# A fused attention and mixture-of-experts kernel: the first stage's unsplit result kept in a buffer of its own, and one more tile made with seven products

## The chip, the cores and the metric

One core of a Trainium2 chip runs the whole kernel in one launch. The metric is the device time in microseconds (us), from the first to the last instruction plus what lies around them. The profile also gives the *span*, the time from the first to the last instruction of one profiled execution.

## The reference, cut to what matters

```python
x = attention(q, k, v, proj)                    # hash-bucket masked, 1536 tokens x 512
x = moe(x, w_gate, w_output_gate, w1, w2)       # 8 experts, relu, 512 -> 1024 -> 512   ("first stage" below)
def _moe2_ref(x, w_a, w_b, w_out):              # ("second stage" below)
    a = x @ w_a                                 # 512 -> 1536
    b = x @ w_b
    return (a * b @ w_out).astype(np.float32)
```

## The kernel before, in words

The kernel has three parts, one behind another: attention, the experts (the first stage here), and the gated product `a * b @ w_out` (the second stage here). The change touches the end of the first stage and the second stage.

**Split operands.** Every matmul works on pairs: a value is written as a rounded high part (`ACT.activation(..., Copy)` into fp32r) plus a low part (value minus high part, on VectorE or GpSimd), and a product is three matmuls, high*high, high*low, low*high (`mm3`, L910 to L913; `product`, L1151; `outp`, L1077).

**The experts** loop over 8 experts `e` and 8 blocks `f`. In each step TensorE does `mm1(e, f)` and then `mm2` of the step before; ScalarE makes the relu's high part (L924), VectorE the low part (L925), and `mm2` needs both one step later. When an expert is done, `y_sum` (one step into the next expert) adds two PSUM halves into `yt`, and `y_store` (two steps in) splits `yt` into its high part `y_h` (four ScalarE copies, L975) and its low part `y_l` (four on VectorE, L976). The last expert is split straight from PSUM by `y_evac` (L957, L958). `y_h` and `y_l` hold 4 blocks of 128 channels by all tokens; GpSimd zeroes them before the first store (L814).

**The second stage** goes over 12 blocks `f` of the 1536 hidden columns, and for each over two halves `c` of 768 tokens: 24 tiles (c, f). For f < 2 a tile is *plain* (`ab`): two token halves `hf` of 384, each 8 weight blocks by 3 matmuls into two PSUM banks, `aba` and `abb`; that is 48 matmuls. From f = 2 on a tile is made with *seven* products (`seven`, a Winograd-type scheme): 7 products by 2 by 3 = 42 matmuls, with VectorE sums between them (L1171, L1175). It alternates the banks from tile to tile (`turn`). Seven products need sums of the activations, `TH` and `TL`, made once for each c by `t_work`: the unsplit value is first put together again as `y_h + y_l` (L1117, `whole`), then come the differences (L1120), the rounded high parts on ScalarE (L1123) and the low parts on VectorE (L1127). The intermediate sums lie in the buffer `accs`, which later holds output sums. They also need sums of the weights (`s_work`, L1142 to L1147).

**Side work.** Each tile has steps in which it hands out other work: `fill(k)` takes one `outp` (three 512-wide matmuls of the output product, for a tile made before), `side(k)` takes what `todo_of` laid down for step k: turning the raw 64-bit weights into floats (`w2_a` on ScalarE, `w2_s` on VectorE, `w2_k` on ScalarE, `w2_b` on VectorE, then the next load on SP's queue), splitting weights (`part`: L881 on ScalarE, L882 on GpSimd; `w2_c` for the output weights), weight sums. In a plain tile `ab` first issues all matmuls of a token half, then the copy of `aba` (L1068), the product with `abb` (L1069), the rounding (L1052), and only then come steps 0 to 2 (first half) or 3 to 6 (second half). A step of a plain tile also takes one item from `todo`, the list of all `t_work` items: 28 steps, 28 items. The low part of `a * b` (L1054, `low`) is issued when the next half's matmuls have been issued.

The order on every engine is the program's order: an instruction that waits holds all behind it on its engine. A buffer that is used again waits for the last use of what it held, also for a use that comes later in the program on another engine.

Of the kernel before, what the change touches and what calls it, by code (L numbers as in the profile page):

```python
# [23 lines left out]
C = 224  # L24
# [9 lines left out]
def attn_moe_kernel(ctx: ExitStack, tc: tile.TileContext, xin, cst, projd, wblk, wmoe, w2in, out):  # L34
# [567 lines left out]
    with tc.manual_schedule():  # L602
# [214 lines left out]
        s2 = ctx_2.enter_context(tc.tile_pool(name="s2", bufs=3, reuse_waits="tile"))  # L817
# [10 lines left out]
        SEQ = [(0, 0), (0, 1), (1, 0), (1, 1), (0, 2)]  # L828
        for m in range(2, 12):
            SEQ += [(m, 0), (m, 1), (m - 1, 2)]  # L830
# [10 lines left out]
        def w2_a(*k):  # L841
            T2[k] = c2.tile([128, 512], F32, tag="t2", name="t2", bufs=5)
            f64_hi(R2[k], T2[k])

        def w2_s(*k):
            X2[k] = c2.tile([128, 512], U32, tag="x2", name="x2")
# [16 lines left out]
        def w2_c(m):  # L863
            t = T2.pop((m, 2))
            h = s2.tile([128, 512], F32R, tag="h2", name="h2")
            l = s2.tile([128, 512], F32R, tag="l2", name="l2")
# [4 lines left out]
        SW = {}  # L871
# [5 lines left out]

        def part(m, nm):
            src = SW[nm] if nm in SW else a_part(m, nm)
            p = s2.tile([128, 2, 256], F32R, tag="pc", name="pc", bufs=9)  # L880
# [103 lines left out]
        def cc_work():  # L984
# [20 lines left out]
            (7, 7): [ids_load],  # L1005
# [3 lines left out]
        for n, (e, f) in enumerate(steps):  # L1009
            mm1(e, f)  # L1010
            if n:
                mm2(*steps[n - 1])
            if f == 0 and e:
                y_sum(e - 1)
            w_split(n + 2, 0)
            w_split(n + 1, 1)
            if f == 1 and e:
                y_store(e - 1)
            if f in (4, 6) and e + 1 < E:
                x_tpose(e + 1, (f // 2 - 2,))  # L1020
            if f == 6 and e + 2 < E:
                x_load(e + 2)
            if e == E - 4 and f in (2, 4, 6):
# [19 lines left out]
        accs = fast.tile([128, 9, 512], F32, name="accs")  # L1043
        af = accs.rearrange("p a b -> p (a b)")
# [13 lines left out]
        def ab(c, f, hf):  # L1058
# [3 lines left out]
            order = [(i, d) for k in range(2) for i in range(2) for d in (2 * k, 2 * k + 1)]  # L1062
            for i, d in order if first else sorted(order):
                    pc = PCS[f, f"{i + 1}{d // 2 + 1}"]
                    wh, wl = (pc[:, k, d % 2 * 128:d % 2 * 128 + 128] for k in range(2))
                    mm3(p[i][:, :384], wh, wl, y_h[:, d, t0:t0 + 384], y_l[:, d, t0:t0 + 384], d == 0, d == 3)
            a = tmp(("c11", "c21")[hf])
            ACT.activation(a, p[0][:, :384], ACTF.Copy)  # L1068
# [5 lines left out]
        def outp(k, f):  # L1074
# [16 lines left out]
            o = accs[:, (k - 6) % 9]  # L1091
            if own:
                o = s2.tile([128, DM], F32, tag="pc", name="osb", bufs=9)
                ACT.activation(o, a, ACTF.Copy, scale=s)
            elif f == 1:
# [15 lines left out]
        def t_work(c):  # L1111
            yh, yl = y_h.bitcast(F32), y_l.bitcast(F32)
            at = ((3072, 0, 768, 1536), (2304, 0, 768, 1536))[c]
            t1, t2, t3, t4 = TF = [af[:, o:o + 768].rearrange("p (a b) -> p a b", a=2) for o in at]

            def whole(o, d, n):
                return lambda: DVE.tensor_tensor(out=o, in0=yh[:, d, n], in1=yl[:, d, n], op=ALU.add)  # L1117

            def tt(o, x, y, op=ALU.subtract):
                return lambda: DVE.tensor_tensor(out=o, in0=x, in1=y, op=op)  # L1120

            def hi(i):
                return lambda: ACT.activation(TH[c][i], TF[i], ACTF.Copy)  # L1123

            def low(i):
                th = TH[c][i].bitcast(F32) if i else yh[:, lo_d, n2[c]]
                return lambda: DVE.tensor_tensor(out=TL[c][i], in0=TF[i], in1=th, op=ALU.subtract)  # L1127

            a, b = n1[c], n2[c]
# [6 lines left out]
        def s_work(m, k):  # L1136
            def new(nm):
                SW[nm] = fast.tile([128, 256], F32, tag=nm, name=nm)
                return SW[nm]

            if k == 0:
                DVE.tensor_tensor(out=new("s1"), in0=a_part(m, "21"), in1=a_part(m, "22"), op=ALU.add)  # L1142
                DVE.tensor_tensor(out=new("s2"), in0=SW["s1"], in1=a_part(m, "11"), op=ALU.subtract)
            elif k == 1:
                DVE.tensor_tensor(out=new("s3"), in0=a_part(m, "11"), in1=a_part(m, "21"), op=ALU.subtract)
            else:
                DVE.tensor_tensor(out=new("s4"), in0=a_part(m, "12"), in1=SW["s2"], op=ALU.subtract)  # L1147
# [15 lines left out]
        def seven(c, m, fill, side, low):  # L1163
# [40 lines left out]
            c21 = add(tmp("c21"), y, p1)  # L1204
# [9 lines left out]
        def todo_of(c, f):  # L1214

            m, w = [[] for _ in range(7)], []
            if c == 0:
                w = [(2, f)]
                if 1 <= f < 11:
                    for k, at in ((0, 4), (1, 4), (2, 5)):  # L1220
                        m[at].append(lambda k=k: s_work(f + 1, k))
            elif f < 10:
                w = [(0, f + 2), (1, f + 2)]
            for k, (i, n) in enumerate(w):
                m[2 * k].append(lambda a=(n, i): w2_a(*a))
                m[2 * k + 1] += [lambda a=(n, i): w2_s(*a), lambda a=(n, i): w2_k(*a)]
                m[2 * k + 2].append(lambda a=(n, i): w2_b(*a))
            if c == 0:
                m[3].append(lambda: w2_c(f))
            elif f < 11:  # L1230
                for k, nm in enumerate(ORDER if f else ("11", "12", "21", "22")):
                    m[k].append(lambda nm=nm: part(f + 1, nm))
# [11 lines left out]
        ts = [t_work(c) for c in range(2)]  # L1244
        todo = ts[0][0] + ts[1][0]
        low = None
        for f in range(12):
            for c in range(2):
# [10 lines left out]
                if f < 2:  # L1259
                    for hf in range(2):  # L1260
                        last, low = low, ab(c, f, hf)
                        if last:
                            last()
                        for k in ((0, 1, 2), (3, 4, 5, 6))[hf]:
                            fill(k)
                            side(k)
                            if todo:
                                todo.pop(0)()
                    if (c, f) == (0, 0):
                        cc_work()  # L1270
                    if f:
                        for g in ts[c][1]:
                            g()
# [70 lines left out]
```

## Time and profile before

| | |
|---|---|
| time, median of 3 runs | 743.83 us (743.38 to 744.12) |
| the profiled execution's own time | 742.49 us |
| its span | 740.7 us |
| TensorE's mean granted clock in it | 0.992 |
| first stage (experts) | to about 435.8 us |
| four plain tiles | about 435.8 to 487.3 us |
| twenty tiles of seven products | from 487.3 us |

A row of a timeline gives the start in us, the duration in us, the engine, the line of the kernel, what is written and read, and in brackets how long the engine sat idle before it and what released it. TensorE's rows overlap, since its matmuls are pipelined: the distance between two starts is the cost of one, the duration is not.

### The profile page before, as it was taken

Reading aid. Unit: us, or ns where it says so; the run is one execution under the profiler, and the core shown is the slowest. Engines: PE = TensorE matmul, PEld = TensorE weight load, DVE = VectorE, ACT = ScalarE, POOL = GpSimd, SP = SyncE. Lnnn points to the kernel's source line nnn. Section 1 sums busy time; section 2 is a strip of 40 time slices with the busy share of each in tenths; the row PEclk is TensorE's granted clock in tenths of the full one; section 3 lists DMA queues with packets and bytes.
Section 4 is the critical chain, followed back from the end, with each engine's and each line's share of the span. In section 5 each row is a group of like instructions: output and inputs, shape, how many; then the busy total and the mean of one; then the engine's idle time right before and its main releaser. Section 6 shows DMA issues by size and latency. Waiting matters only on the chain.

```text
span 740.7 us, 13120 instructions
## 1 busy us (share of the span) xinstructions
PE 715.0 (97%) x4561; PEld 612.0 (83%) x4562; DVE 554.2 (75%) x1099; ACT 439.6 (59%) x929; POOL 223.0 (30%) x261
## 2 busy tenths in 40 slices
PE   8899999999999999999999998799999999999995
PEld 6676777776776789999999997788999999999994
DVE  6778777888776678777778858866777777777653
ACT  6878777777777357666677745456443453434311
POOL 3233232333533283212210002133223332233215
PEclk9999999999999999999999999899999999999998
DMA  7357351321301068888898612121212212120003
GB/s 239 118 214 262 102 167 58 105 69 66 134 8 60 15 223 241 241 188 243 267 238 275 209 30 85 38 78 57 86 35 80 86 58 86 33 81 31 1 30 145
DMA packets 42681, 88.48 MB, mean 119 GB/s; under 512 B 7328, under 2 KB 10736, under 8 KB 42608
## 3 DMA queue, kind: packets, MB, share of 16 engines
q1 hardware_dynamic: 39936, 81.07, 35.5%
q0 software_dynamic: 2304, 6.31, 2.3%
q8 instruction: 38, 0.62, 0.4%
q14 instruction: 35, 0.29, 0.1%
q10 hardware_dynamic: 368, 0.20, 0.1%
HBM read 73.32 MB, written 13.12 MB: 117 GB/s over the span
## 4 chain that ended last, share of the span: by engine, by line
PE 79%; DVE 7%; issue 6%; ACT 3%; POOL 3%; DMA 2%; SPq 0%; POOLq 0%; ACTq 0%; DVEq 0%
PE tp L186 9%; PE av L201 8%; PE y L951 6%; PE s L158 4%; PE s L159 4%; PE h L913 4%; PE h L912 3%; PE h L911 3%; PE y L952 3%; PE aba L1156 3%; PE abb L1156 3%; PE aba L1158 3%; PE aba L1157 3%; PE abb L1158 3%; PE abb L1157 3%
## 5 line engine op out<-in xcount | busy, mean ns | idle before, releaser
L164 DVE TENSOR_REDUCE mm<-s 128x1 f32<-128x768 f32 x96 | 91.1, 949 | 25.1 <-PE s L159 24.1
L173 ACT ACTIVATE p<-s,sb 128x768 f32<-128x768 f32 x96 | 94.8, 988 | 21.7 <-DVE sb L165 21.0
L186 PEld LDWEIGHTS tp<-cs,p 128*128 128x128 f32 x576 | 64.2, 140 | 36.7 <-ACT p L173 23.4
L485 DVE TENSOR_TENSOR wl<-wr,wh 128x512 fp32r<-128x512 f32 x125 | 81.5, 692 | 8.4 <-ACT wh L484 3.1
L186 PE MATMUL tp<-cs,p 128*128 128x128 f32 x576 | 82.2, 279 | 4.8 <-ACT p L173 3.9
L190 ACT ACTIVATE pt<-tp 128x384 f32<-128x384 f32 x143 | 64.9, 487 | 32.6 <-PE tp L186 32.6
L484 ACT ACTIVATE wh<-wr 128x512 fp32r<-128x512 f32 x128 | 73.7, 623 | 3.2 <-DMA wr<-wmoe 3.0
L951 PE MATMUL y<-hl,wh 128*128 128x448 f32 x224 | 74.8, 377 | 0.1
L158 PE MATMUL s<-tk,tq 76*128 76x384 f32 x192 | 73.1, 381 | 0.3 <-DVE tq L135 0.3
L911 PE MATMUL h<-xh,wh 128*128 128x224 f32 x256 | 71.5, 279 | 0.2 <-ACT xh L418 0.2
L913 PE MATMUL h<-xh,wl 128*128 128x224 f32 x256 | 70.7, 276 | 0.2 <-DVE wl L485 0.2
L912 PE MATMUL h<-xl,wh 128*128 128x224 f32 x256 | 70.3, 274 | 0.3 <-DVE xl L419 0.3
L882 POOL TENSOR_TENSOR pc<-t,pc 128x256 fp32r<-128x256 f32 x38 | 30.0, 791 | 128.8 <-ACT pc L881 59.8
L201 PE MATMUL av<-pt,v 128*64 128x384 f32 x360 | 68.0, 499 | 0.2 <-DVE r L225 0.2
L1052 ACT ACTIVATE gh<-c 128x384 fp32r<-128x384 f32 x28 | 14.7, 526 | 88.2 <-DVE c L1175 67.8
L159 PE MATMUL s<-bk,bq 128*128 128x384 f32 x192 | 65.1, 339 | 0.0
L952 PE MATMUL y<-hl,wl 128*128 128x224 f32 x224 | 59.6, 266 | 0.0
L911 PEld LDWEIGHTS h<-xh,wh 128*128 128x128 f32 x256 | 49.0, 191 | 1.3 <-ACT xh L418 0.4
L913 PEld LDWEIGHTS h<-xh,wl 128*128 128x128 f32 x256 | 49.2, 192 | 0.4 <-DVE wl L485 0.4
L912 PEld LDWEIGHTS h<-xl,wh 128*128 128x128 f32 x256 | 49.2, 192 | 0.5 <-DVE xl L419 0.5
L201 PEld LDWEIGHTS av<-pt,v 128*64 128x64 f32 x360 | 21.9, 136 | 32.7 <-issue 24.5
L882 POOL TENSOR_TENSOR pc<-s,pc 128x256 fp32r<-128x256 f32 x40 | 36.0, 910 | 42.8 <-ACT pc L881 42.8
(235 smaller groups left out, 1921.9 us busy)
## 6 DMA issues: line engine op xcount, KB each, us to landing
wr<-wmoe SPq DMA_DIRECT2D x128, 256.0 KB
r<-w2in SPq DMA_DIRECT2D x36, 512.0 KB
x<-xin SPq DMA_DIRECT2D x30, 384.0 KB
xr<-zero SPq DMA_DIRECT2D x13, 512.0 KB
xg<-xr SPq DMA_DIRECT2D x14, 256.0 KB
v<-xin SPq DMA_DIRECT2D x16, 192.0 KB
wb<-wblk SPq DMA_DIRECT2D x1, 640.0 KB
x<-xin SPq DMA_DIRECT2D x3, 192.0 KB
```

The costliest lines, as they stand in the source:

```text
L158: PE.matmul(p[:, c, :384], T[h, 0][:76, qs], T[h, 1][:76, sl], start=True, stop=False)
L159: PE.matmul(p[:, c, :384], B[h, 0][:, qs], B[h, 1][:, sl], start=False, stop=True)
L164: DVE.tensor_reduce(out=m[:, 1:2], in_=st[g][:, :, :384], axis=AX.XY, op=ALU.min)
L173: ACT.activation(p.rearrange("p (c n) -> p c n", c=2), st.pop(g)[:, :, :384], ACTF.Exp, scale=scl.pop(g), bias=nbs.pop(g), accum_out=sums[ ...
L186: PE.transpose(ps[:, j * 128:(j + 1) * 128], pt_[g][:, k * 128:(k + 1) * 128], ident)
L201: PE.matmul(av[h][c * 64:(c + 1) * 64, :384], v, PT[h][:, k, c * 384:(c + 1) * 384], start=(k == 0), stop=(k == NT - 1), skip_group_check= ...
L485: eng.tensor_tensor(out=l, in0=r, in1=h.bitcast(F32), op=ALU.subtract)
L911: PE.matmul(ps, wh, xh, start=first, stop=False)
L912: PE.matmul(ps, wh, xl, start=False, stop=False)
L913: PE.matmul(ps, wl, xh, start=False, stop=last)
L951: PE.matmul(p, wh[:, w], hl, start=(f == 0), stop=False, skip_group_check=True)
L952: PE.matmul(p[:, 0], wl[:, w], hl[:, 0], start=False, stop=(f == 7), skip_group_check=True)
```

## The change: what it does

1. A third buffer `y_w` of the shape of `y_h` takes the unsplit first-stage result. Four more memsets on GpSimd zero it; `y_store` gets four more ScalarE copies for each of the first seven experts, and two ScalarE copies from PSUM serve the last.
2. `t_work` works in place on `y_w`: the sums `whole` go, and one difference fewer is made. The buffer `accs` goes; its output sums lie in parts of `y_w` that are no longer needed (`AT`).
3. The tile (0, 1) is made with seven products instead of plain. So the weight sums of block 1 are made at the end of the first stage (steps (7, 6) and (7, 7)), block 1 has eight weight parts instead of four, and the list `todo` is replaced by places written out by hand in `todo_of` for the tiles (0, 0), (1, 0), (0, 1), (1, 1) and (0, 2).
4. In a plain tile the steps are spread: the copy of `aba` is issued as soon as its last matmul is issued, then, in the middle of the matmuls, the `low` of the half before and step 0 or 3 (`mid`); steps 1, 2 or 4 to 6 come behind the rounding. The very first half calls `mid` behind its matmuls.
5. Buffers are smaller or elsewhere: raw weights 3 to 2, converted weights 5 to 4, sign bits 2 to 1, weight parts 9 in one pool to 4 + 5 in two. The order of weight loads (`SEQ`) and of `part` changes. `p1` also serves as the product buffer of the second half and of `c21`. One output sum (block 1, k = 4) is scaled on VectorE instead of ScalarE.

The diff, cut to its core (new tile pools and the moved `s_work`, `pc_tile` as described above are left out):

```diff
-        for y in (y_h, y_l):
+        y_w = yp.tile([128, 4, N + C], F32, name="y_w")
+        for y in (y_h.bitcast(F32), y_l.bitcast(F32), y_w):
             for d in range(4):
-                POOL.memset(y.bitcast(F32)[:, d], 0.0)
-        r2 = ctx_2.enter_context(tc.tile_pool(name="r2", bufs=3, reuse_waits="tile"))
+                POOL.memset(y[:, d], 0.0)
+        r2 = ctx_2.enter_context(tc.tile_pool(name="r2", bufs=2, reuse_waits="tile"))
...
-            T2[k] = c2.tile([128, 512], F32, tag="t2", name="t2", bufs=5)
+            T2[k] = c2.tile([128, 512], F32, tag="t2", name="t2", bufs=4)
...
-            w2_load(SEQ.index(k) + 3)
+            w2_load(SEQ.index(k) + 2)
...
             for d in range(4):
-                y = YS.pop((e, d))
+                y = YS[e, d]
                 ACT.activation(y_h[:, d, sl], y, ACTF.Copy)
                 DVE.tensor_tensor(out=y_l[:, d, sl], in0=y, in1=y_h.bitcast(F32)[:, d, sl], op=ALU.subtract)
+            for d in range(4):
+                ACT.activation(y_w[:, d, sl], YS.pop((e, d)), ACTF.Copy)
...
+            (7, 6): [lambda: s_work(1, 0)],
+            (7, 7): [ids_load, lambda: s_work(1, 1), lambda: s_work(1, 2)],
...
             y_evac(E - 1, i)
+        for i in range(2):
+            src = Y[E - 1][i].rearrange("p (a b) -> p a b", a=2)[:, :, :C]
+            ACT.activation(y_w[:, 2 * i:2 * i + 2, bass.ds(o_regs[E - 1], C)], src, ACTF.Copy)
...
-        def ab(c, f, hf):
+        def ab(c, f, hf, mid):
...
+            a = tmp(("c11", "p1")[hf])
             for i, d in order if first else sorted(order):
...
-            a = tmp(("c11", "c21")[hf])
-            ACT.activation(a, p[0][:, :384], ACTF.Copy)
+                if (i, d) == (0, 3):
+                    ACT.activation(a, p[0][:, :384], ACTF.Copy)
+                    if not first:
+                        mid()
+            if first:
+                mid()
...
+            elif f == 1 and k == 4:
+                DVE.tensor_scalar(out=o, in0=a, scalar1=s, scalar2=None, op0=ALU.mult)
...
+            w = (y_w[:, lo_d, a], y_w[:, hi_d, b], y_w[:, lo_d, b], y_w[:, hi_d, a])
...
             return [
-                whole(t3, lo_d, b), whole(t1, lo_d, a), tt(t1, t3, t1), whole(t2, hi_d, b), tt(t3, t2, t3),
-                tt(t2, t2, t1), tt(t4, yh[:, hi_d, a], t2), tt(t4, t4, yl[:, hi_d, a], ALU.add), hi(1),
-                hi(2), low(1), hi(3), low(2), low(3),
-            ], [hi(0), low(0)]
+                tt(w[0], w[2], w[0]), tt(w[2], w[1], w[2]), tt(w[1], w[1], w[0]), tt(w[3], w[3], w[1])
+            ] + [g(i) for i in (1, 2, 3, 0) for g in (hi, low)]
...
-            c21 = add(tmp("c21"), y, p1)
+            c21 = add(p1, y, p1)
...
+            if f < 3:
+                t, u = t_work(0), t_work(1)
+            if (c, f) == (0, 0):
+                before.extend(t[:3])
+                conv(0, 2, 0, 1, 1, 2)
+                for k, g in ((1, t[3]), (2, t[4]), (3, u[0]), (5, t[6]), (5, t[5])):
+                    put(k, g)
+                put(4, w2_c, 0)
+                for k, nm in ((0, "11"), (2, "s2"), (3, "12"), (4, "s3"), (6, "s1")):
+                    put(k, part, 1, nm)
+            elif (c, f) == (1, 0):
+                conv(1, 2, 0, 1, 1, 2)
+                for k, g in ((0, t[7]), (1, t[8]), (2, t[9]), (3, t[10]), (4, t[11])):
+                    put(k, g)
+                put(3, w2_c, 1)
+                for k, nm in ((4, "22"), (5, "s4"), (6, "21")):
+                    put(k, part, 1, nm)
+                put(6, cc_work)
+            elif (c, f) == (0, 1):
+                for k, g in ((0, u[1]), (1, u[2]), (2, u[3]), (5, u[4]), (6, u[6])):
+                    put(k, g)
+                conv(2, 0, 3, 4, 4, 5)
+            elif (c, f) == (1, 1):
+                conv(2, 1, 0, 1, 1, 2)
+                for k, g in ((0, u[5]), (1, u[7]), (3, u[8]), (4, u[9]), (6, u[10])):
+                    put(k, g)
+                for k in range(3):
+                    put(2 + k, s_work, 2, k)
+                conv(3, 0, 4, 5, 5, 6)
+                for k, nm in ((2, "11"), (3, "12"), (4, "s2"), (5, "s3"), (5, "s1"), (6, "22"), (6, "s4")):
+                    put(k, part, 2, nm)
...
-                if f < 2:
+                if f < 2 and (c or not f):
...
                     for hf in range(2):
-                        last, low = low, ab(c, f, hf)
-                        if last:
-                            last()
-                        for k in ((0, 1, 2), (3, 4, 5, 6))[hf]:
-                            fill(k)
-                            side(k)
-                            if todo:
-                                todo.pop(0)()
+                        def mid(last=low):
+                            if last:
+                                last()
+                            step(3 * hf)
+
+                        low = ab(c, f, hf, mid)
+                        for k in ((1, 2), (4, 5, 6))[hf]:
+                            step(k)
```

## Rows read from the trace of the kernel before

**Rows 1.** The page's part 1: busy time, share, instructions of each engine.
```profile
PE 715.0 (97%) x4561; PEld 612.0 (83%) x4562; DVE 554.2 (75%) x1099; ACT 439.6 (59%) x929; POOL 223.0 (30%) x261
```
**Rows 2.** Stretches: from:to, length, busy time and count of each engine, granted clock, DMA.
```profile
478.00:482.00 4.00, 4.00 (x13) 3.71 (x12) 1.14 (x3) 4.00 (x8) 2.21 (x3) 0.50 0.32 93
524.00:547.00 23.00, 23.00 (x121) 21.11 (x120) 18.15 (x33) 10.28 (x22) 6.88 (x8) 1.00 0.24 69
```
**Rows 3.** Timeline of TensorE, the plain tiles and the first of seven products.
```profile
435.87 0.42 PE L911 MATMUL aba<-y_h,pc 128*128 128x384 f32 x1
...
444.86 0.34 PE L911 MATMUL aba<-y_h,pc 128*128 128x384 f32 x1
...
451.00 0.34 PE L913 MATMUL aba<-y_h,pc 128*128 128x384 f32 x1
451.83 0.44 PE L911 MATMUL abb<-y_h,pc 128*128 128x384 f32 x1 [0.49 <-DVE c L1069]
...
453.88 0.34 PE L913 MATMUL abb<-y_h,pc 128*128 128x384 f32 x1
457.29 0.45 PE L911 MATMUL aba<-y_h,pc 128*128 128x384 f32 x1 [3.06 <-ACT c L1068]
...
473.12 0.40 PE L1086 MATMUL q<-l,gh 128*128 128x512 f32 x1
477.29 0.79 PE L1087 MATMUL q<-h,gl 128*128 128x512 f32 x1 [3.78 <-DVE gl L1054]
...
483.52 0.34 PE L913 MATMUL abb<-y_h,pc 128*128 128x384 f32 x1
...
485.27 0.39 PE L1085 MATMUL q<-h,gh 128*128 128x512 f32 x1
...
487.11 0.39 PE L1087 MATMUL q<-h,gl 128*128 128x512 f32 x1
487.33 0.33 PE L1156 MATMUL aba<-y_h,pc 128*128 128x384 f32 x1
...
491.57 0.44 PE L1156 MATMUL aba<-y_h,pc 128*128 128x384 f32 x1 [0.57 <-ACT p L1185]
...
494.50 0.44 PE L1156 MATMUL abb<-th,pc 128*128 128x384 f32 x1 [0.92 <-DVE u L1171]
...
500.93 0.34 PE L1156 MATMUL abb<-y_h,pc 128*128 128x384 f32 x1
...
503.09 0.44 PE L1156 MATMUL aba<-th,pc 128*128 128x384 f32 x1 [0.25 <-DVE u L1171]
```
**Rows 4.** Group of one line and shape, 433 to 501 us: busy, mean ns.
```profile
L1117 DVE TENSOR_TENSOR accs<-y_h,y_l 128x768 f32<-128x768 f32 x6 | 5.7, 951 | 0.0
```
**Rows 5.** Timeline of VectorE, then of GpSimd, in the plain tile (1, 0).
```profile
447.31 2.92 DVE L1120 TENSOR_TENSOR accs<-accs 128x768 f32<-128x768 f32 x2
...
447.10 1.33 POOL L868 TENSOR_TENSOR l<-t,h 128x512 fp32r<-128x512 f32 x1 [32.19 <-ACT h L867]
```
**Rows 6.** Timeline of ScalarE at two expert boundaries, and TensorE and VectorE at the last.
```profile
291.26 0.36 ACT L924 ACTIVATE hl<-h 128x224 fp32r<-128x224 f32 x1 [1.26 <-PE h L913]
...
419.81 1.22 ACT L975 ACTIVATE y_h<-yt 128x224 f32 x4
420.93 0.33 ACT L924 ACTIVATE hl<-h 128x224 fp32r<-128x224 f32 x1
...
422.27 0.37 PE L943 MATMUL y<-hl,wh 128*128 128x224 f32 x1
...
421.83 0.38 DVE L925 SCALAR_TENSOR_TENSOR hl<-h,hl 128x224 fp32r<-128x224 f32 x1
```
**Rows 7.** Timeline of GpSimd as the first stage begins and at the first seven-product tile.
```profile
274.65 6.10 POOL L814 MEMSET y_l<- 128x1760 f32 x4
288.38 0.51 POOL L1028 COPY spare<-hl 128x1 f32<-128x1 f32 x1 [7.63 <-DVE hl L925]
...
488.31 2.43 POOL L882 TENSOR_TENSOR pc<-s,pc 128x256 fp32r<-128x256 f32 x2 [6.03 <-ACT pc L881]
```

More of the change, by code (lines that the diff above doesn't have):

```diff
@@ L869, in w2_c, with pc_tile @@
             W2[m] = h, l
-        SW = {}
+        SW, pcs = {}, [0]
+        def pc_tile(shape, dt, nm):
+            pcs[0] += 1
+            return (s2 if (pcs[0] - 1) % 9 < 4 else fast).tile(shape, dt, tag="pc", name=nm, bufs=4 if (pcs[0] - 1) % 9 < 4 else 5)
         A = {"11": (0, 0), "12": (0, 256), "21": (1, 0), "22": (1, 256)}
@@ L876, in a_part, with s_work, new @@
             return T2[m, i][:, o:o + 256]
+        def s_work(m, k):
+            def new(nm):
+                SW[nm] = s2.tile([128, 256], F32, tag=nm, name=nm, bufs=1)
+                return SW[nm]
+            if k == 0:
+                DVE.tensor_tensor(out=new("s1"), in0=a_part(m, "21"), in1=a_part(m, "22"), op=ALU.add)
+                DVE.tensor_tensor(out=new("s2"), in0=SW["s1"], in1=a_part(m, "11"), op=ALU.subtract)
+            elif k == 1:
+                DVE.tensor_tensor(out=new("s3"), in0=a_part(m, "11"), in1=a_part(m, "21"), op=ALU.subtract)
+            else:
+                DVE.tensor_tensor(out=new("s4"), in0=a_part(m, "12"), in1=SW["s2"], op=ALU.subtract)
         def part(m, nm):
             src = SW[nm] if nm in SW else a_part(m, nm)
-            p = s2.tile([128, 2, 256], F32R, tag="pc", name="pc", bufs=9)
+            p = pc_tile([128, 2, 256], F32R, "pc")
             ACT.activation(p[:, 0], src, ACTF.Copy)
@@ L1090, in outp @@
             a, s = acc.pop(k), cc[:, k:k + 1]
-            o = accs[:, (k - 6) % 9]
+            if not own:
+                d, at = AT[k - 3]
+                o = y_w[:, d, at:at + 512]
             if own:
-                o = s2.tile([128, DM], F32, tag="pc", name="osb", bufs=9)
+                o = pc_tile([128, DM], F32, "osb")
                 ACT.activation(o, a, ACTF.Copy, scale=s)
+            elif f == 1 and k == 4:
+                DVE.tensor_scalar(out=o, in0=a, scalar1=s, scalar2=None, op0=ALU.mult)
             elif f == 1:
@@ L1111, in t_work @@
         def t_work(c):
[L1112 to L1120, printed above, removed]
+            a, b = n1[c], n2[c]
@@ L1129, in t_work @@
-            a, b = n1[c], n2[c]
+                th = TH[c][i].bitcast(F32) if i else y_h.bitcast(F32)[:, lo_d, b]
+                return tt(TL[c][i], w[i], th)
             return [
-                whole(t3, lo_d, b), whole(t1, lo_d, a), tt(t1, t3, t1), whole(t2, hi_d, b), tt(t3, t2, t3),
-                tt(t2, t2, t1), tt(t4, yh[:, hi_d, a], t2), tt(t4, t4, yl[:, hi_d, a], ALU.add), hi(1),
-                hi(2), low(1), hi(3), low(2), low(3),
-            ], [hi(0), low(0)]
[L1136 to L1147, printed above, removed]
+                tt(w[0], w[2], w[0]), tt(w[2], w[1], w[2]), tt(w[1], w[1], w[0]), tt(w[3], w[3], w[1])
+            ] + [g(i) for i in (1, 2, 3, 0) for g in (hi, low)]
@@ L1228, in todo_of, with conv, put @@
-            if c == 0:
-                m[3].append(lambda: w2_c(f))
+            m = [[] for _ in range(7)]
+            def conv(n, i, *at):
+                for k, g in zip(at, (w2_a, w2_s, w2_k, w2_b)):
+                    m[k].append(lambda g=g: g(n, i))
+            def put(k, g, *a):
+                m[k].append(lambda: g(*a))
+            if f < 3:
[29 more added lines that the diff above has]
+                    put(k, part, 2, nm)
+            elif c == 0:
+                if f == 2:
+                    put(0, u[11])
+                    conv(3, 1, 0, 1, 1, 2)
+                conv(f, 2, *((2, 3, 3, 4) if f == 2 else (0, 1, 1, 2)))
+                put(5 if f == 2 else 3, w2_c, f)
+                if f < 11:
+                    for k, at in ((0, 4), (1, 4), (2, 5)):
+                        put(at, s_work, f + 1, k)
@@ L1230, in todo_of @@
             elif f < 11:
-                for k, nm in enumerate(ORDER if f else ("11", "12", "21", "22")):
-                    m[k].append(lambda nm=nm: part(f + 1, nm))
+                for i in range(2 * (f < 10)):
+                    conv(f + 2, i, *((0, 1, 1, 2), (2, 3, 3, 4))[i])
+                for k, nm in enumerate(("11", "12", "s2", "s3", "s1", "22", "s4")):
+                    put(k, part, f + 1, nm)
             return m
@@ L1242, in units @@
             return [(k, i) for k in range(3) for i in (f - 2, f - 1) if i >= 0]
-        ts = [t_work(c) for c in range(2)]
-        todo = ts[0][0] + ts[1][0]
-        low = None
+        low, before = None, []
         for f in range(12):
@@ L1257, in side, with step @@
                         g()
[L1259 to L1273 removed]
+                if f < 2 and (c or not f):
+                    def step(k):
+                        fill(k)
+                        side(k)
+                    for g in before:
+                        g()
+                    before = []
+                    for hf in range(2):
+                        def mid(last=low):
[5 more added lines that the diff above has]
+                            step(k)
                 else:
```

41 lines of the change are left out of this document (14 added, 27 removed).

## The prediction

> **What bounds the kernel now.** I read the page's busy times first. TensorE is busy 97% of the span, nobody else over 83% [rows 1], so only two things shorten the kernel: fewer or faster matmuls, and TensorE's gaps. The stretches come next. In the steady tiles TensorE is busy 23.00 of 23.00 us while ScalarE has 10.28 and GpSimd 6.88 [rows 2]: there is nothing to win there but matmuls, and there is cover for other engines' work. The losses lie between 435.87 us, the first matmul of the second stage, and 500.93, where the second seven-product tile begins: 65.06 us for five tiles [rows 3].
>
> TensorE's timeline prices them. At full pace 36 matmuls of 384 columns start between 444.86 and 451.00: 6.14 / 35 = 0.175 us each. Nine of 512 columns start between 485.27 and 487.11: 0.23 each. Four plain tiles and one of seven products are 192 + 42 = 234 of the first kind (41.04 us at 0.1754), and the `outp` units in them are 0 + 0 + 3 + 6 + 6 = 15 of three 512-wide matmuls (10.35 us), together 51.39. So 13.67 us are lost [rows 3]:
>
> - 0.57 at the start: the first tile takes 8.99 us to 444.86 instead of 48 x 0.1754 = 8.42.
> - 0.65 at 451.83, the bank `abb` waiting for the product L1069 (0.83 between the starts, less 0.18).
> - 3.24 at 457.29, `aba` waiting for the copy L1068 (3.41 less 0.18). The copy stands on ScalarE behind the conversions, parts and rounded sums of the steps before.
> - 3.94 at 477.29, an output matmul waiting for the low part L1054, which stands on VectorE behind `todo`'s sums (4.17 less 0.23).
> - 2.85 by the clock behind that gap: from 477.29 to 483.52 TensorE does 4 x 0.23 + 14 x 0.1754 = 3.38 us of work in 6.23 us. The granted clock in 478 to 482 is 0.50, the lower of its two levels, 1.2 GHz [rows 2]. The gap of 3.24 us was not followed by slow matmuls; the one of 3.94 was.
> - 2.09 in tile (0, 2): 13.60 us from 487.33, against 42 x 0.1754 + 18 x 0.23 = 11.51. The waits at 491.57 (copy `p1`) and 494.50 (a sum on VectorE) are most of it.
> - The last 0.33 is slow first matmuls after waits.
>
> **The change part by part.**
>
> *Seven products for (0, 1).* 48 matmuls become 42: 6 x 0.1754 = 1.05 us less. The full pace of the five tiles is then 228 x 0.1754 + 10.35 = 50.34 us.
>
> *Sums in place, copies earlier.* The six sums L1117 and two of the differences L1120 go: 8 x 0.95 = 7.6 us of VectorE [rows 4], out of the stretch in which VectorE and ScalarE run late. The copy of `aba` is queued ahead of the steps instead of behind, so in (1, 0) only what is left over from the half before stands ahead of it, and the half has 12 more matmuls (2.1 us) before the bank is wanted. The low part of a half is issued in the middle of the next half, ahead of its side work. I therefore count the waits at 451.83, 457.29 and 477.29 as gone, and the slow clock with the last: 0.65 + 3.24 + 3.94 + 2.85 = 10.68. The 0.57 at the start stays: it is the last expert's split.
>
> *New waits, by place.* (a) The end of (0, 1). Its last product lies in `aba`, and the plain tile behind it, (1, 1), wants `aba` first. In the trace a seven-product tile is followed by another with the banks swapped: at 500.93 the next tile starts on `abb`, and `aba` comes free only at 503.09, behind a product, a rounding, a low part and a sum. Had it been wanted at 500.93, the wait would have been 2.16 [rows 3]. I take 2.1. It would be 0.9 if only the last sum were outstanding (0.34 for the matmul's end and about 0.55 for the sum, less nothing hidden), and 3.0 if a GpSimd operation of 1.33 us [rows 5] holds VectorE for most of it. (b) In (0, 1) the copy `p1` now also waits for the low part of (1, 0), since both use the buffer `p1`; behind it on ScalarE is nothing that is due soon, but the third product waits for the copy. The nearest row is the same wait in (0, 2), 0.57 idle [rows 3]. Here ScalarE has three parts ahead of it, there it had more: 0.4, from 0 to 1.2. (c) (0, 2) keeps its kind of load: ScalarE brings conversions, five parts and a rounded sum from (1, 1) into it, ahead of `p1`. 1.6 instead of 2.09, from 1.1 to 2.5. (d) Anything else in (1, 0) and (1, 1): 0.3, from 0 to 1.5.
>
> VectorE and GpSimd hold each other up: two sums L1120 took 2.92 us together instead of 1.9, the second of them while GpSimd's operation of 1.33 us ran from 447.10 [rows 4, 5]. The Trainium skill (SBUF — State Buffer, section "SBUF: two separate sides") says why: an operation of VectorE with two SBUF inputs and one of GpSimd that reads SBUF exclude each other for their whole length. This trace agrees. By the rule alone the four added parts on GpSimd would each cost VectorE their length just where `p1` waits, and (b) would stand at its upper end; the time would then be 0.8 us longer.
>
> *The copies into `y_w`.* Four more per expert boundary on ScalarE, 1.12 us (420.93 - 419.81) ahead of the next relu [rows 6]. At the first boundaries ScalarE sat idle 1.26 us before the relu after that, which takes it up. At the last one it does not: the relu at 420.93 is late already, and TensorE's matmul at 422.27 follows VectorE's low part (421.83 + 0.38) at once. With the copies the relu starts at 422.05 and ends at 422.38, the low part at about 422.8, the matmul at about 422.87: 0.6 us lost. From 0 to 1.5. The two copies at the very end lie beside the first plain tile; ScalarE's next work there is 4 us away.
>
> *Free of cost, with their cover.* Four more memsets take 6.1 us on GpSimd and end at about 286.9, before GpSimd's next work at 288.38 [rows 7]; without that cover the first store would wait. The weight sums of block 1 run on VectorE in the last steps of the first stage, whose weights are all split by then. A raw weight load has at least four steps from issue to use also with two buffers; at 69 GB/s for a 0.24 share of the DMA engines [rows 2] I estimate 0.52 MB at 1.8 us. One output sum moved to VectorE is 0.7 us in place of a similar one on ScalarE. With four buffers for converted weights, ScalarE waits in eight later tiles for GpSimd's part "12"; see the rivals.
>
> *The sum.* 50.34 + 0.57 + 2.1 + 0.4 + 1.6 + 0.3 = 55.31 us for the five tiles, 9.75 less than 65.06; less 0.6 at the expert boundary, 9.15. The profiled execution took 742.49 us, so 733.3; the median of the runs is 1.34 higher: **734.7 us**.
>
> **The rivals.**
>
> - *The clock falls again.* If (a) or (b) grows to a gap like the one of 3.94 us, TensorE pays 1.9 more and again 2.85: 739.4. For it: two GpSimd parts in a row took 2.43 us [rows 7] and would add to (a). Against: the 3.24 us gap did not do it, and nothing in my order exceeds 2.2.
> - *Every boundary pays.* If the copies hold the relu at the other six boundaries as well, 6 x 1.12 = 6.7 us come back: 741.4. Against: the 1.26 us of idle time [rows 6].
> - *The other side: converted weights with four buffers.* In tiles (1, 2) to (1, 9) the conversion `w2_a` of the second weight block takes the buffer that the part "12", one step before, still reads on GpSimd. ScalarE stands, and with it the parts and conversions behind, then VectorE's `w2_s` and the sums that free TensorE's banks. It decides from 9.15 / 8 = 1.14 us of TensorE's time in a tile. If GpSimd has two parts to do then (2.43) and only the one step's slack of about 0.9 is there, each tile loses 1.5 and the time is 734.7 + 12 = 746.7. For it: both engines collide. Against: ScalarE is busy only 10.28 of 23.00 us in these tiles [rows 2], and GpSimd 6.88.
> - *Better than forecast.* No wait but (a), at 0.9, and (c) at 1.1, and none at the boundary: 50.34 + 0.57 + 2.0 = 52.91, 12.15 less, 731.7.
>
> **How the numbers follow.** The forecast, between 731.7 and about 738, has 0.78; the clock 0.09; every boundary 0.04; four buffers 0.05; still better 0.04. The upper end with all waits at their upper bounds is 50.34 + 0.57 + 3.0 + 1.2 + 2.5 + 1.5 = 59.11, 5.95 less, and 1.5 at the boundary: 739.4, which takes in the clock's case. Range 731.7 to 739.4. About 0.2% (1.5 us) is what a measurement of this kernel tells from no change. Every case but the four buffers ends further below than that; with a little for mild forms of it near no change: faster 0.92, same 0.02, slower 0.06.
>
> **What would show it.** Right: 42 matmuls in (0, 1); no gap over 2.5 us and no stretch at 0.50 clock between 435 and 500 us; a wait of about 2 us as (1, 1) begins, released by VectorE's sum; 0.6 us at the last expert boundary; steady tiles of 11.5 us as before; the second seven-product tile's end (1, 2) some 9 us earlier. Wrong: a wait in tiles behind (1, 2) that recurs, a late first matmul of an expert step at each boundary, or a new gap near 4 us with slow matmuls behind it.

## The result, and the profile after

The changed kernel takes 732.71 us (median of 4 runs, 732.04 to 734.76); the kernel before took 743.87 (743.38 to 744.12) beside it. The ratio is 0.9856, with a 95% interval from 0.9835 to 0.9876: faster by 1.4%, 2.0 us below the forecast of 734.7 and inside its range. The profiled execution took 732.93 us. Its span is 731.2 us, 9.5 less than before.

The page's busy times and granted clock, against [rows 1]:

```profile
span 731.2 us, 13193 instructions
...
PE 710.0 (97%) x4555; PEld 607.8 (83%) x4556; DVE 554.0 (76%) x1101; ACT 448.3 (61%) x962; POOL 233.6 (32%) x269
...
PEclk9999999999999999999999999999999999999998
```

The stretches of the kernel after: the first two tiles, then (0, 1), (1, 1) and (0, 2), and a stretch of two steady tiles. The columns are those of [rows 2].

```profile
436.61:454.13 17.52, 17.27 (x96) 16.88 (x97) 14.68 (x20) 12.59 (x25) 6.68 (x6) 1.00 0.15 42
454.13:466.32 12.19, 9.87 (x53) 8.80 (x52) 11.26 (x18) 5.30 (x11) 4.99 (x4) 1.00 0.15 47
466.32:478.99 12.67, 12.67 (x66) 11.90 (x67) 8.02 (x14) 6.40 (x13) 1.80 (x2) 1.00 0.20 65
478.99:491.65 12.66, 11.80 (x61) 10.65 (x60) 9.73 (x19) 8.67 (x18) 4.97 (x5) 1.00 0.42 123
514.70:537.70 23.00, 23.00 (x120) 21.00 (x119) 18.10 (x34) 10.30 (x22) 6.97 (x8) 1.00 0.24 69
```

The five tiles take 436.61 to 491.65 = 55.04 us instead of 65.06; the forecast was 55.31. The clock is 1.00 throughout, where a stretch at 0.50 lay in [rows 2]. The steady tiles are as before, 11.5 us each. The next rows are TensorE's waits between 255 and 735 us, with the total in us, how many there were, and the longest:

```profile
PE aba L930 <- DVE u L1184: 1.8, 1, 1.8
PE abb L1169 <- ACT p L1198: 0.9, 1, 0.9
PE aba L1169 <- ACT p L1198: 0.5, 1, 0.5
PE y L970 <- DVE hl L944: 0.4, 2, 0.3
...
PE y L959 <- ACT hl L943: 0.3, 1, 0.3
PE aba L931 <- DVE y_l L977: 0.2, 1, 0.2
```

The first is new: it is (1, 1) waiting for the bank that (0, 1) leaves last. The second and third are the copies `p1` of (0, 2) and (0, 1). The wait for `y` at L959 is the last expert boundary, the last row the second stage's start. Their places in TensorE's timeline, the rows that answer to [rows 3] and [rows 6]:

```profile
422.58 0.37 PE L959 MATMUL y<-hl,wh 128*128 128x224 f32 x1 [0.27 <-ACT hl L943]
...
457.39 0.40 PE L1116 MATMUL p<-h,gl 128*128 128x512 f32 x1
458.30 0.45 PE L1169 MATMUL aba<-y_h,pc 128*128 128x384 f32 x1 [0.52 <-ACT p L1198]
...
466.32 0.44 PE L930 MATMUL aba<-y_h,pc 128*128 128x384 f32 x1 [1.80 <-DVE u L1184]
...
483.51 0.44 PE L1169 MATMUL abb<-y_h,pc 128*128 128x384 f32 x1 [0.86 <-ACT p L1198]
```

The waits for the product L1069, the copy L1068 and the low part L1054, which cost 0.65, 3.24 and 3.94 us before, are gone. The wait at 458.30 shows VectorE and GpSimd holding each other up again. Rows of VectorE, ScalarE and GpSimd just before it:

```profile
454.88 1.70 DVE L1149 TENSOR_TENSOR y_l<-y_w,y_h 128x768 fp32r<-128x768 f32 x1
456.50 0.70 DVE L1006 TENSOR_TENSOR cc<-ids 128x12 f32<-128x12 f32 x1
457.12 0.55 DVE L1078 TENSOR_TENSOR gl<-p,gh 128x384 fp32r<-128x384 f32 x1
```

```profile
457.76 0.49 ACT L1198 ACTIVATE p<-aba 128x384 f32<-128x384 f32 x1 [1.32 <-DVE gl L1078]
```

```profile
454.47 1.29 POOL L869 TENSOR_TENSOR l<-t,h 128x512 fp32r<-128x512 f32 x1 [2.63 <-ACT h L868]
455.96 1.21 POOL L901 TENSOR_TENSOR pc<-t,pc 128x256 fp32r<-128x256 f32 x1 [0.20 <-ACT pc L900]
```

The low part of 768 columns takes 1.70 us beside GpSimd, the same shape alone 0.95; the small product `cc` behind it takes 0.70, where it took 0.17 in the kernel before. Behind both the low part `gl` comes late, and with it the copy that frees TensorE, as (b) of the forecast said. VectorE's rows ahead of the wait at 466.32 are the chain that (a) named, a product, a low part and a sum, with a weight conversion while ScalarE rounds:

```profile
464.09 0.56 DVE L1188 TENSOR_TENSOR p<-c,p 128x384 f32<-128x384 f32 x1
464.56 0.68 DVE L860 SCALAR_TENSOR_TENSOR t<-t,x 128x512 uint32<-128x512 uint32 x1
465.24 0.56 DVE L1078 TENSOR_TENSOR gl<-p,gh 128x384 fp32r<-128x384 f32 x1
465.71 0.55 DVE L1184 TENSOR_TENSOR u<-aba,u 128x384 f32<-128x384 f32 x1
```

The sum needs only the matmuls, the last of which started at 464.18; it is late because it is issued behind the low part. Issuing it ahead would be another cure, which was not tried.

### The profile page after: what moved, and what is told of

Same layout as the page of the kernel before. It is cut to its first block, busy times and chain, and to the rows that moved or that the text cites. A ratio compares the mean times of both kernels' runs of the same rounds, so it can differ in the third digit from the quotient of the medians.

```text
span 731.2 us, 13193 instructions
## 1 busy us (share of the span) xinstructions
PE 710.0 (97%) x4555; PEld 607.8 (83%) x4556; DVE 554.0 (76%) x1101; ACT 448.3 (61%) x962; POOL 233.6 (32%) x269
## 5 line engine op out<-in xcount | busy, mean ns | idle before, releaser
L901 POOL TENSOR_TENSOR pc<-t,pc 128x256 fp32r<-128x256 f32 x38 | 33.2, 878 | 158.2 <-ACT pc L900 143.6
L1076 ACT ACTIVATE gh<-p 128x384 fp32r<-128x384 f32 x24 | 12.6, 526 | 72.1 <-DVE p L1188 68.2
L851 ACT ACTIVATE x<-r 128x512 uint8<-128x512 uint8 x36 | 28.5, 792 | 32.3 <-DVE x L848 32.3
```

## The experiments

All times are medians. The kernel before ran beside each group: 743.68 us beside the first four, 742.85 beside the next four, 742.89 beside the last three. Kernels of different groups are best compared by their distance from the kernel before. Line numbers shift a little from kernel to kernel.

**1. The bank wait taken away.** Only the plain tile (1, 1) takes its banks in the other order.

```diff
-            p = [pa.tile([128, 512], F32, tag="ab" + "ab"[i], name="ab" + "ab"[i]) for i in range(2)]
+            ab_of = "ba" if (c, f) == (1, 1) else "ab"
+            p = [pa.tile([128, 512], F32, tag="ab" + ab_of[i], name="ab" + ab_of[i]) for i in range(2)]
```

> The changed kernel with the two banks swapped in the plain tile (1, 1) alone, so that it begins on the bank that the tile (0, 1) left first. Theory 'new wait': the changed kernel waits 1.96 us there (466.32 us, released by VectorE's sum), and nothing else is hidden behind it: that wait goes, the five tiles take about 53.1 us instead of 55.04, the time falls by about 1.9 us to 730.8. Rival 'moved on': VectorE and ScalarE are late by as much, the wait only moves to the next bank or into (0, 2), and the time stays within 0.5 us of 732.7.

Measured: 730.98 us, ratio to before 0.9843 (0.9823 to 0.9862); five tiles 436.74 to 489.75 = 53.01 us. The row where the wait stood, and the one before it:

```profile
464.32 0.34 PE L1172 MATMUL aba<-y_h,pc 128*128 128x384 f32 x1
464.49 0.34 PE L930 MATMUL abb<-y_h,pc 128*128 128x384 f32 x1
```

No idle time is left between the tiles, and 2.03 us of the five tiles went with it. The new wait is what (a) said: it came from which bank (1, 1) wants first.

**2. The tile (0, 1) plain again**, with in-place sums and spread steps kept.

```diff
-            (7, 6): [lambda: s_work(1, 0)],
-            (7, 7): [ids_load, lambda: s_work(1, 1), lambda: s_work(1, 2)],
+            (7, 7): [ids_load],
...
-                for k, nm in ((0, "11"), (2, "s2"), (3, "12"), (4, "s3"), (6, "s1")):
+                for k, nm in ((0, "11"), (3, "12"), (4, "21"), (6, "22")):
...
-                if f < 2 and (c or not f):
+                if f < 2:
```

The plain tile here reads columns of `y_h` and `y_l` (two channel blocks of its second token half) in which a step of (1, 0) has already put a rounded sum, so one operand is partly replaced; the work and its order are those of a plain tile.

> The changed kernel with (0, 1) plain again, and so without the weight sums and the four extra weight parts of block 1; sums in place and spread steps stay. Theory 'order of the queues': the seven products give 6 x 0.1754 = 1.05 us and cost their own waits, 0.5 us in (0, 1) and 1.96 us behind it; without them the time is 1.4 us lower, 731.3. Rival 'seven products': the tile carries the gain, also by relieving the output sums that follow; the time is above 735.

Measured: 731.0 us, 0.9839 (0.9821 to 0.9858); five tiles 53.20 us. So seven products in (0, 1), put in as the change does, lose more than they save: 1.96 us at the bank and 0.68 at their own copy `p1`, against 1.05 of matmuls.

**3. The steps handed out as before**, in-place sums and seven products kept.

```diff
-                if (i, d) == (0, 3):
-                    ACT.activation(a, p[0][:, :384], ACTF.Copy)
-                    if not first:
-                        mid()
...
+            ACT.activation(a, p[0][:, :384], ACTF.Copy)
...
-                        low = ab(c, f, hf, mid)
-                        for k in ((1, 2), (4, 5, 6))[hf]:
+                        last, low = low, ab(c, f, hf)
+                        if last:
+                            last()
+                        for k in ((0, 1, 2), (3, 4, 5, 6))[hf]:
```

> The changed kernel with the steps of the plain tiles handed out as before: all matmuls of a half, then the copy, the product and the rounding, then the steps. Sums in place and seven products for (0, 1) stay. Theory 'order of the queues': the waits for the copy and for the low part come back in part, 3 to 6 us, 736 to 739, with gaps of 2 to 4 us in TensorE's timeline between 445 and 480 us. Rival 'VectorE': with 7.6 us of sums gone the order does not matter, below 734.

Measured: 741.31 us (10 runs, 739.41 to 744.53), 0.9981 (0.9965 to 0.9998); five tiles 62.88 us. This is worse than either theory gave. TensorE's longer gaps in its timeline:

```profile
461.36 0.45 PE L1164 MATMUL aba<-y_h,pc 128*128 128x384 f32 x1 [1.84 <-ACT p L1193]
...
469.62 0.45 PE L930 MATMUL aba<-y_h,pc 128*128 128x384 f32 x1 [1.80 <-DVE u L1179]
...
490.19 0.45 PE L1164 MATMUL abb<-y_h,pc 128*128 128x384 f32 x1 [1.77 <-ACT p L1193]
```

and two stretches behind the second and third of them:

```profile
470.00:474.00 4.00, 4.00 (x16) 4.00 (x15) 0.16 (x1) 1.75 (x3) 0.00 (x0) 0.57 0.04 16
491.00:494.00 3.00, 3.00 (x11) 2.70 (x10) 1.51 (x3) 1.98 (x4) 1.41 (x2) 0.50 0.17 25
```

Unspread, TensorE waits 1.8 us for the copy `p1` in each of the two seven-product tiles, and it runs at the lower of its two levels, 1.2 GHz, after the second and third gap. Each slow stretch costs some 1.55 us (from 470.25 to 474.08, 3.83 us for 13 matmuls of 0.1754), so 3.1 of the 7.84 us by which the five tiles are longer than the changed kernel's are the clock's. The second gap is the bank wait, which the changed kernel has as well. What is left, 4.7 us, is within the 3 to 6 that the first theory gave to the waits. With seven products, the spreading is needed.

**4. Only the spreading, on the kernel before**, without `y_w` and with the plain tile (0, 1).

```diff
-        def ab(c, f, hf):
+        def ab(c, f, hf, mid):
...
+                if (i, d) == (0, 3):
+                    ACT.activation(a, p[0][:, :384], ACTF.Copy)
+                    if not first:
+                        mid()
+            if first:
+                mid()
```

> The kernel before with the spread steps alone: the copy of the first bank, the low part and step 0 or 3 in the middle of a half's matmuls; sums by putting high and low part together, four plain tiles. Theory 'order of the queues': the waits at 451.83 and 457.29 us go (3.9 us), the one at 477.29 with its slow clock (6.8 us) goes too unless VectorE's 7.6 us of sums fill the queue: 733 to 740. Rival 'VectorE': without the sums in place VectorE stays late, above 741.

Measured: 735.79 us, 0.9896 (0.9873 to 0.9919); five tiles 58.63 us, no stretch at the lower clock. The waits left are of the old kind, a bank and a low part:

```profile
457.53 0.44 PE L911 MATMUL aba<-y_h,pc 128*128 128x384 f32 x1 [1.82 <-ACT c L1069]
...
474.95 0.50 PE L1092 MATMUL q<-h,gl 128*128 128x512 f32 x1 [1.30 <-DVE gl L1054]
```

The order alone brings 7.9 us. VectorE is busy for 49.66 us of these five tiles, where it is for 40.31 in experiment 2. That kernel differs by the in-place sums, and also by the smaller buffers and the side work placed by hand.

**5. The in-place sums without the other two parts**: (0, 1) plain, steps as in 3, and the rounded sum that would spoil (0, 1) moved behind it. The smaller buffers and the side work placed by hand stay.

```diff
...
-                for k, g in ((0, t[7]), (1, t[8]), (2, t[9]), (3, t[10]), (4, t[11])):
+                for k, g in ((0, t[7]), (1, t[8]), (2, t[9])):
...
-                for k, g in ((0, u[1]), (1, u[2]), (2, u[3]), (5, u[4]), (6, u[6])):
+                for k, g in ((0, u[1]), (1, u[2]), (2, u[3]), (5, u[4]), (6, u[6]), (6, t[10])):
...
```

> The changed kernel with both other parts undone: (0, 1) plain, steps handed out behind all matmuls of a half; only the buffer y_w, the sums in place and the smaller buffers stay. The rounded sum that overwrites y_h is made behind (0, 1). Theory 'order of the queues': the copy of the first bank still stands behind the steps, so gaps of 1 to 3 us stay in TensorE's timeline, and the time is 737 to 742. Rival 'VectorE': the sums were the cause, below 735.

Measured: 735.22 us, 0.9894 (0.9879 to 0.9909); five tiles 59.12 us. My expectation missed (the rival, below 735, narrowly too): the in-place sums, with the buffers and places that come with them, bring 7.6 us, about as much as the order alone. No run separates the sums from those places. The two cures overlap, since 7.9 + 7.6 is more than the 12.7 of experiment 2, which has both. Either one makes a late copy or low part less late, and both together remove the three old waits. The longest wait of this kernel, 1.84 us for a copy `p1`, is followed by slow matmuls as well:

```profile
484.99 0.45 PE L1163 MATMUL aba<-y_h,pc 128*128 128x384 f32 x1 [1.84 <-ACT p L1192]
...
486.00:489.00 3.00, 3.00 (x10) 2.71 (x10) 1.29 (x3) 1.77 (x4) 1.20 (x2) 0.52 0.21 34
```

Beside 3, this kernel differs by the plain tile (0, 1) and the moved sum. It is 7.6 us below the kernel before, where 3 is 2.4 below: unspread, the seven products are a loss of about 5 us, in which the bank wait and one more slow stretch are counted.

**6. The copies into `y_w` one step later** than the high parts, from (e, 1) to (e, 2).

```diff
+        def y_keep(e):
+            sl = bass.ds(o_regs[e], C)
             for d in range(4):
                 ACT.activation(y_w[:, d, sl], YS.pop((e, d)), ACTF.Copy)
...
+            if f == 2 and e:
+                y_keep(e - 1)
```

> The changed kernel with the four copies into y_w one step later, (e, 2) instead of (e, 1). Theory: they delay the relu only at the last expert boundary; there the relu starts 1.12 us earlier, no matmul of the first stage waits for it, and the time falls by 0.6 us, to 732.1. Rival: the copies cost where they are put, wherever that is, and the time stays at 732.7 or rises.

Measured: 732.57 us, 0.9864 (0.9849 to 0.9879), not to be told from the changed kernel. Its trace has no wait at the last boundary, so what was expected of the boundary is there. But in this execution the bank wait is followed by slow matmuls:

```profile
464.44 0.44 PE L930 MATMUL aba<-y_h,pc 128*128 128x384 f32 x1 [1.81 <-DVE u L1189]
464.73 0.34 PE L931 MATMUL aba<-y_l,pc 128*128 128x384 f32 x1
...
465.79 0.52 PE L931 MATMUL aba<-y_l,pc 128*128 128x384 f32 x1
466.10 0.52 PE L932 MATMUL aba<-y_h,pc 128*128 128x384 f32 x1
```

The matmuls from 465.79 to 468.98, ten in all, run at a granted clock of 0.50, and the five tiles take 56.59 us instead of 55.04. Experiment 9 takes this up.

**7. Swapped banks and late copies together** (1 and 6).

> Both small cures together: banks of (1, 1) swapped, copies into y_w one step later. Theory: two waits that have nothing to do with each other add up, 1.7 + 0.6 = 2.3 us below the changed kernel, 730.4. Rival: one wait hides the other, 731 or more.

Measured: 730.27 us, 0.983 (0.9817 to 0.9844); five tiles 52.98 us, clock 1.00. This is as expected, and below the changed kernel and the kernel before.

**8. The tile (0, 1) plain, spread, in place, late copies**, with the rounded sum moved as in 5.

> (0, 1) plain, spread steps, sums in place, copies into y_w one step later; the rounded sum that overwrites y_h is made behind (0, 1), since that tile still reads it. Theory: 731.0 with (0, 1) plain less 0.6 at the boundary, 730.4, the same as with seven products and swapped banks within 0.5 us. Rival: with its waits cured the seven-product tile is ahead by its 1.05 us, and this kernel is at 731.4 or more.

Measured: 731.46 us, 0.9844 (0.9829 to 0.9858), at the edge of what the rival gave; five tiles 54.17 us. With its bank wait cured, the version with seven products is ahead by 54.17 - 52.98 = 1.19 us; the times, 731.46 and 730.27, say the same. This is near the 1.05 of the six matmuls, but it does not come from there. The tile (0, 1) takes 10.50 us plain (453.13 to 463.63) and 10.20 with seven products in experiment 11, the kernel of 7 again (453.03 to 463.23): 0.30 less, since the wait for `p1` takes back most of the 1.05. The tile (0, 2) takes 13.70 us here and 12.67 there, with this wait in it:

```profile
481.75 0.44 PE L1173 MATMUL aba<-y_h,pc 128*128 128x384 f32 x1 [1.13 <-ACT p L1202]
```

In experiment 2, with the rounded sum where the change has it, (0, 2) takes 12.73 us, and the five tiles, 53.20, are only 0.19 above those of experiment 1. So most of the 1.19 us is the price of moving the rounded sum and its low part behind (0, 1), which a plain tile needs to read whole operands; the seven products themselves bring 0.2 to 0.3.

**9. The changed kernel once more.**

> The changed kernel once more, beside the version with swapped banks and late copies on the same chip. Time 732.7 again. Open is whether its bank wait of about 1.8 us idle, behind the tile (0, 1), is followed by slow matmuls (granted clock 0.50). Theory 'the clock decides from one execution to the next': the instructions ahead of the wait stand within 0.1 us of where they stood, and yet the five tiles take either about 55.0 us (no slow matmuls) or about 56.6 (some 3 us of slow ones), and runs scatter over 2 to 3 us. Rival 'the place decides': always 55.0, and never a slow matmul there in this kernel; the scatter has another source.

Measured: 733.98 us (732.12 to 734.79, 4 runs), 0.9871 (0.9852 to 0.989). The profiled execution, 734.79 us, has the wait of the first profile to the hundredth, and behind it what the first had not:

```profile
466.44 0.44 PE L930 MATMUL aba<-y_h,pc 128*128 128x384 f32 x1 [1.80 <-DVE u L1184]
466.72 0.33 PE L931 MATMUL aba<-y_l,pc 128*128 128x384 f32 x1
...
467.30 0.52 PE L931 MATMUL aba<-y_l,pc 128*128 128x384 f32 x1
467.62 0.52 PE L932 MATMUL aba<-y_h,pc 128*128 128x384 f32 x1
```

The stretch of the slow ones, and the five tiles:

```profile
467.30:470.28 2.98, 2.98 (x10) 2.89 (x9) 1.43 (x2) 1.10 (x3) 0.00 (x0) 0.50 0.01 6
...
436.74:493.34 56.60, 53.17 (x273) 49.73 (x274) 43.69 (x68) 32.96 (x64) 18.45 (x17) 0.97 0.21 66
```

One program, one gap of 1.80 us, and five tiles of 55.04 us in one execution and 56.60 in the other. These 1.56 us are most of the 1.86 by which the two executions differ. The rival, that the place decides, is ruled out: the lower clock comes in one execution and not in the other.

**10. The bank wait made longer** by one more VectorE difference of 0.95 us.

```diff
+            if (c, m) == (0, 1):
+                t_work(0)[5]()
             c12 = add(u2, x, u2)
```

> The changed kernel with one more VectorE difference of 768 columns (0.95 us) ahead of the last sum of the tile (0, 1); it writes again what is there already. The bank wait grows from 1.8 us idle to about 2.75. Theory 'a longer gap brings the lower clock more surely': slow matmuls behind it, five tiles 55.0 + 0.95 + 1.5 to 2.9 = 57.5 to 58.9 us, time 735 to 736.5. Rival 'only the gap counts': 56.0 us, no slow matmuls, time 733.7.

Measured: 734.83 us (6 runs, 734.09 to 738.79), 0.9905 (0.9884 to 0.9925). Its profiled execution, 734.29 us:

```profile
466.76 0.44 PE L930 MATMUL aba<-y_h,pc 128*128 128x384 f32 x1 [2.67 <-DVE u L1184]
467.04 0.34 PE L931 MATMUL aba<-y_l,pc 128*128 128x384 f32 x1
...
436.19:492.10 55.91, 51.62 (x273) 48.23 (x274) 44.91 (x69) 32.96 (x64) 18.42 (x17) 1.00 0.22 66
```

The gap is 0.87 us longer, the five tiles 0.87 us, and no matmul is slow. A longer gap did not bring the lower clock in this execution, where the rival's 56.0 us hold. The median lies 0.85 above the changed kernel's in the same group, about what the gap grew by. Two of the six runs, 736.74 and 738.79 us, had mean granted clocks of 0.994 and 0.991 against 0.997 in the other four. Where the clock fell in them was not recorded, so the theory that a longer gap brings it more surely stays open: a mean of 0.993 was also seen in the profiled execution of experiment 7, with 1.00 in its five tiles.

**11. The version of 7 once more, beside 9 and 10.**

> Swapped banks in the tile (1, 1) and copies into y_w one step later, once more, on the same chip as the changed kernel. 2 to 2.5 us below the changed kernel (about 730.3 against 732.7), five tiles 53.0 us, no slow matmuls between the first stage and the end. If the bank wait were paid back later: no difference between the two.

Measured: 730.26 us (729.8 to 730.72), 0.9829 (0.9816 to 0.9843), 3.7 below the changed kernel in the same group; five tiles 52.97 us:

```profile
435.50:488.47 52.97, 51.35 (x273) 48.30 (x274) 43.68 (x68) 32.85 (x64) 18.42 (x17) 1.00 0.23 70
```

The five tiles are 2.07 us below the 55.04 of one profile of the changed kernel and 3.63 below the 56.60 of the other; the last boundary comes on top. This version, in 7 and here, is the fastest tried.

## Why the prediction was right, point by point

- **Full pace.** TensorE's pace did not change and (0, 1) has 42 matmuls. Full pace 50.34 us by the forecast's sum; the five tiles took 55.04, so 4.70 were lost. The places below add up to 4.58; the other 0.11 is the first matmul behind the wait in (0, 1), 0.29 us to the next start (458.30 to 458.59) instead of 0.18.
- **The start**, forecast 0.57. The first two tiles take 17.52 us for 96 x 0.1754 = 16.84, so 0.68 with all else in them. (d), forecast 0.3, is 12.67 - (48 x 0.1754 + 18 x 0.23 = 12.56) = 0.11 in (1, 1), its first matmul behind the bank wait (466.32 to 466.60), and nothing told apart from the start in (1, 0).
- **(a) the bank wait**, forecast 2.1. Start to start it is 466.32 - 464.18 = 2.14, less 0.18: 1.96. Experiment 1 took it away and gained 2.03. Reading the wait from the banks of [rows 3], as if (1, 1) had been there, held.
- **(b) `p1` in (0, 1)**, forecast 0.4: 0.91 between starts, less 0.23, is 0.68. It was mis-sized, within its bounds. The trace puts it down to VectorE and GpSimd holding each other up, which the forecast named as its upper side; no run took this away. The Trainium skill (SBUF — State Buffer, section "SBUF: two separate sides") has an operation of VectorE with two SBUF inputs and one of GpSimd that reads SBUF exclude each other; the low part of 1.70 us, 0.95 alone, which began while GpSimd's 1.29 us ran, agrees. Of the two sums of [rows 5] it was the first that GpSimd held up, with 1.93 us from 447.31, and not the second, as the forecast has it; the 2.92 us of both stand.
- **(c) the tile (0, 2)**, forecast 1.6: 12.66 - 11.51 = 1.15, near its lower bound. Before, it held two waits, for `p1` (0.57 idle) and for VectorE's sum (0.92) [rows 3]. The first grew to 0.86: ScalarE's copy starts 3.98 us into the tile (482.97) instead of 3.70. The second is gone, and so it is in experiments 2 and 5, which have the sums in place, while 4, which has not, keeps 0.48 of it. I had sized the wait as one of ScalarE's queue; what shrank was VectorE's.
- **The old waits** (10.68 us) are gone, as counted. I had put each to one queue. Experiments 4 and 5 show that either the order or the relief of VectorE (with the buffers and places that come with it) brings some three fifths of the 12.7 us alone, and neither removes all.
- **The copies into `y_w`**, forecast 0.6 at the last boundary: the first stage's part from the first expert matmul to 436.61 took 176.74 us instead of 176.14. The relu L943 starts at 422.19, counted from the first expert matmul 1.12 later than in [rows 6], the length of the four copies. With these one step later the part took 176.02 and 176.08 us in experiments 7 and 11. Experiment 6 took the wait away as well, but there the part took 175.28, which is shorter than the wait explains. The other boundaries cost nothing.
- **Four buffers**, the other side: no wait of TensorE's in the tiles behind (1, 2), and the stretch of two steady tiles is 23.00 us as before. That rival is ruled out. Between 490 and 720 us no wait of ScalarE's for GpSimd is listed. Its waits there are led by these:

```profile
ACT gh L1076 <- DVE p L1188: 67.7, 20, 6.0
ACT gh L1076 <- DVE u L1188: 31.1, 20, 2.0
```

- **The median.** Net I had 9.15 us off the profiled execution, and the two profiled spans differ by 9.5. The rest of the 2.0 is the step from a profiled execution to a median: I added 1.34 us because before's profiled execution lay that far below its median, while after's lay 0.22 above. The second set of runs, at 733.98, is 0.7 below the forecast. That the five tiles came so near, 55.04 against 55.31, is partly luck: (b) was 0.28 too low and (c) 0.45 too high, and the execution profiled beside the result had no slow matmuls, where the one of experiment 9 took 56.60.
- **The clock** is where the argument was too simple. I gave 0.09 to a fall of the clock and tied it to a gap like the one of 3.94 us; that nothing in the new order exceeds 2.2 us was to count against it. Experiment 9 shows it behind 1.80 us in one of two profiled executions of the same kernel, for 1.56 us. So the wait (a) costs 1.96 us or some 3.5, by execution, and part of the kernel's scatter is that. Another part lies ahead: the profiled executions of experiments 7 and 11, one kernel, take 732.20 and 729.80 us and differ by 2.26 us already at the first expert matmul (261.68 and 259.42).

## What to carry to other kernels

When a tile is made in another way, look at which accumulator it releases last and which one its successor wants first: here the tile saved 1.05 us of matmuls, lost 0.68 at its own copy and 1.96 at the bank, and exchanging two names won the 1.96 back. Late work on in-order queues can be cured by issuing it earlier or by taking work off the queue ahead of it; try each alone before adding up their gains, since they overlap. When two versions differ by what you expected, look in which tile the difference lies: the 1.19 us of experiment 8 lay in another one. Price a gap on TensorE at more than its length, as a slow stretch may follow it in some executions.

## What the runs showed of the hardware that was not expected

TensorE's granted clock fell to 0.50, 1.2 GHz, behind idle gaps of 1.8 us in experiments 3, 5, 6 and 9, for ten matmuls and about 1.5 us of loss in the last two. It stayed at 1.00 behind the same gap in the first profile of the changed kernel, behind 2.67 us in experiment 10, and behind 3.06 us in the kernel before [rows 3]. The slow matmuls do not begin at the gap's end: in experiment 9 they begin 0.86 us behind it, in experiment 6 1.35. VectorE's rows ahead of the gap in experiment 6 differ from those of the first profile by one shift of 1.87 us, to within 0.01. What decides it from execution to execution is not settled by these runs.
